# The last expert's remaining product rows: padded stationaries, no zero products, five ScalarE instructions

## The chip, the cores and the metric

The kernel runs on one core of one Trainium2 chip. The metric is the device time of one execution in microseconds (us); times are given as the median of several runs, and one further execution was profiled. The engines are TensorE (PE in the profile, with PEld for its weight loads), VectorE (DVE), ScalarE (ACT), GpSimd (POOL) and SyncE (SP).

## What is computed

Attention over 4 batches of 8 heads (768 positions, 64 columns each) with a causal mask in some heads and a sink-and-window mask in the others, and then a soft mixture of experts on its output. Only the second part bears on the change:

```python
logits = x @ phi                                  # 3072 x 32 slots
d = np.exp(logits - logits.max(0, keepdims=True)); d /= d.sum(0, keepdims=True) + 1e-09
slot_input = (d.T @ x).reshape(8, 4, 512)         # 8 experts, 4 slots each
for e in range(8):
    h = np.maximum(slot_input[e] @ w1[e], 0.0)    # 4 x 1024
    slot_out[e] = h @ w2[e]                       # 4 x 512
c = np.exp(logits - logits.max(1, keepdims=True)); c /= c.sum(1, keepdims=True) + 1e-09
return c @ slot_out.reshape(32, 512)              # 3072 x 512
```

## The kernel before

The program is a list of operations, each with a name, the engines it may run on, estimated costs, what it depends on and which buffers it takes and frees. A planner places them greedily by estimated start and a key, and emits each engine's instructions in that order; an engine then runs its instructions strictly in that order, and waits on semaphores for the others. Buffers in PSUM are five: two pairs of banks "sc", two banks "tr", one pair "pv". The planner also chooses the engine of an operation that allows two.

Attention runs over 16 pairs of batch and head group; GpSimd issues the loads of q, k, v and of the experts' matrices on one queue, so the matrices w1 and w2 arrive one after the other behind the attention's inputs. The last matrix, w2 of expert 7, comes in two pieces: row groups 0 to 5 (piece a) and 6 to 7 (piece b; FL is 6).

The tail, from the last attention pair on, goes so, with the lines of the profile:

- RC and RWR (L897, L898, L906): VectorE sums the exponentials into `rcs`, inverts it, and inverts the row sums into `rrow`.
- H, HR, TH, HE (L930, L940, L952, L279): the first expert layer for four experts at a time, the ReLU on ScalarE, the transposes, and the copies of the hidden rows into `hT_t` (tile xT), which VectorE does.
- W2.0 to W2.7 (L968): the second layer. Each expert's eight row groups are products of a stationary of only 32 columns (four slots of each of eight tiles), put into one of four column groups of the array, so that four run side by side; they add up in four 32-row strips of one "pv" bank. W2.7 does row groups 0 to 5 of the last expert, W2b later 6 and 7.
- SOa (L977): ScalarE scales the bank by `rcs` into `slot_out_a`, without row groups 6 and 7. SOb (L979): the same with them, on VectorE, into `slot_out`, after W2b.
- HG, GP, GE (L989, L999, L277 and L279): for the first 512 output rows the missing two row groups are brought in another way: the hidden rows times the exponentials, as a stationary `gT`.
- OG (L1027) and OM (L1023): the output products. For the first 512 rows an OG pair (gT with piece b) and an OM with `slot_out_a` add up in one bank; all later OM read `slot_out`.
- OE (L1041 on ScalarE, L1043 on VectorE): a bank is scaled by `rrow` into SBUF. ST (L1062): SyncE issues ten stores, four of 256 KB, two of 512 KB, four of 1 MB, each when its OE are done.

An order written out by hand (`seq`, L1052) chains OG and OM of the first rows, W2b and OM.1.0 on TensorE. Between W2.6 and W2.7 the two GP products stand.

After planning, products of a zero tile are put ahead of TensorE operations before which the plan has a gap, so that TensorE isn't idle (`zeros_for`, L1131). The count comes from the gap, and for operations whose name begins with "W2" it is at most 6:

```python
us, w = gap - (1.5 if o.name[:2] == "W2" else 0.12), 512 - c0
before[o.name] = (min(max(0, int(us / (w / 2400))), 6 if o.name[:2] == "W2" else 3), 0, bank, c0)
```

In the tail that puts five zero products of 512 columns, into the second "pv" bank, between GP and W2.7.

Of the kernel before, what the change touches and what calls it, by code (L numbers as in the profile page):

```python
# [15 lines left out]
ACT = mybir.ActivationFunctionType  # L16
# [159 lines left out]
def kernel(  # L176
# [13 lines left out]
    nc = tc.nc  # L190
    P = 128
    B, H, S, D = q.shape
# [22 lines left out]
    elg = sb.tile([P, 6, 4, NS], BF16, name="elg")  # L215
# [9 lines left out]
    rcs = sb.tile([P, 1], F32, name="rcs")  # L225
# [3 lines left out]
    thr = sb.tile([P, 2, H], F32, name="thr")  # L229
# [21 lines left out]
    pvb = ps.tile([P, 2, 512], F32, name="pv")  # L251

    def tr_bf(s, n):
        return trb[s].bitcast(BF16)[:, 0:n]
# [8 lines left out]
    NGT, FL, SOB = 4, 6, "DVE"  # L263
# [4 lines left out]
    hT_t = [xbf[:, 1024 * e:1024 * (e + 1)].rearrange("p (f c) -> p f c", f=8) for e in range(2)]  # L268

    pl = Plan({"S8": 11, "QT": 2, "KT": 2, "VT": 1, "VB": 2, "VF": 3, "PT": 2, "PTX": 2, "XB": 2,  # L270
               "XT": 1, "SC": 2, "TR": 2, "PV": 1})
# [3 lines left out]
    def copy(o, dst, src):  # L275
        if o.eng == "ACT":
            nc.scalar.copy(dst, src)  # L277
        else:
            nc.vector.tensor_copy(dst, src)  # L279
# [44 lines left out]
    NW, UNEVEN = 2 * NE, 5  # L324
    wbuf = [Buf("S8") for _ in range(NW)]
    wland = [None] * NW
    late_mem, last_lands = {}, []

    def w_view(i):
        m = late_mem[i]() if i in late_mem else slots[wbuf[i].slot][:, :]  # L330
        return m.rearrange("p (a f) -> p a f", a=4 if i < NE else 8)
# [84 lines left out]
    def head_mask(h):  # L416
        nc.vector.tensor_scalar(msk[:, h, 0:256], edist[:, 0:256], thr[:, 0, h:h + 1], None, op0=ALU.is_lt)
        nc.vector.tensor_scalar(msk[:, h, 256:896], edist[:, 256:896], thr[:, 1, h:h + 1], None, op0=ALU.is_lt)
# [54 lines left out]
    for n in range(4):  # L473
        o_hm[n] = [pl.op(f"hm{n}.{i}", {"DVE": 0.55}, -28.5 if n == 0 else T * n - 2.0, deps=[o_fl],
                         emit=lambda o, h=n + 4 * i: head_mask(h)) for i in range(2)]
# [15 lines left out]
    def emit_ph3(o):  # L491
        for n in range(4):
# [7 lines left out]
                  emit=lambda o: nc.vector.tensor_copy(phi.rearrange("p n s -> p (n s)"), tr_bf(phs[1].slot, 128)))  # L500
# [110 lines left out]
    def evs(x, b, n):  # L611
        if b == 0:
            return ev[x, b]
        return [e for r0, r1, e in ev[x, b] if r0 < 24 * (n + 1) and r1 > 24 * n]
# [15 lines left out]
    def mask_emit(b, n, m):  # L630

        def f(o):
            pT, mh = pTs[PTb[b, n].slot], msk[:, n::4, :]
            if m < 2:
                pw = pT[:, :, 1024 * m:1024 * (m + 1)].rearrange("p i (g c) -> p i g c", g=2)[:, :, :, 0:256]
                mw = (mh[:, :, 0:768].rearrange("p h (g c) -> p h g c", g=2)[:, :, :, 0:256] if m == 0 else
                      mh[:, :, 384:896].rearrange("p h (g c) -> p h g c", g=2))
            else:
                pw, mw = pT[:, :, 1920:2304], mh[:, :, 256:640]
            nc.vector.tensor_tensor(pw, pw, mw, op=ALU.mult)  # L640
        return f
# [6 lines left out]
    for b in range(B):  # L648
        for n in range(4):
            p = 4 * b + n  # L650
# [4 lines left out]
            def emit_v2(o, n=n, tr=tr):  # L655
                t = tr_bf(tr.slot, 768)
                for j in range(6):
# [4 lines left out]
                      emit=emit_v2)  # L662

            def emit_vb(o, b=b, n=n, tr=tr):
# [4 lines left out]
                           need=[VBb[b]], rel=[tr], emit=emit_vb)  # L669
            VFb[p] = Buf("VF")  # L670

            def emit_vf(o, b=b, n=n, p=p):
# [4 lines left out]
                           emit=emit_vf)  # L677

            PTb[b, n] = Buf("PT")
            for kk, g in enumerate(GORDER):  # L680
# [19 lines left out]
                if g in (1, 3, 4):  # L700
                    m = {1: 0, 3: 1, 4: 2}[g]
                    masko[p, m] = pl.op(f"MK.{p}.{m}", {"DVE": [0.70, 0.70, 0.57][m]}, key + 0.3,
                                        deps=[expo[p, x] for x in ((0, 1), (2, 3), (3, 4))[m]] + o_hm[n],
                                        emit=mask_emit(b, n, m))

        for ns in ([(0, 1), (2, 3)] if b == 0 else [(0, 1, 2, 3)]):
            sc = Buf("SC")

            def emit_lx(o, b=b, sc=sc, ns=ns):
# [4 lines left out]
                      deps=list(dict.fromkeys(e for n in ns for x in "qk" for e in evs(x, b, n))),  # L714
# [13 lines left out]
    xto, lgo, elo, elc, dso, eto = {}, {}, {}, {}, {}, {}  # L728
    dsm = {}
    for b in range(B):  # L730
        for n in range(4):
            p = 4 * b + n
# [4 lines left out]
            for i in iorder:  # L737
                deps, need = [v2e[p], vfo[p]], set()
# [6 lines left out]
                def emit_pv(o, b=b, n=n, p=p, i=i):  # L745
                    pT = pTs[PTb[b, n].slot]
                    vb = vbs[VBb[b].slot]
                    for h in range(2):
                        for j in range(i + 1):
# [3 lines left out]
                            else:  # L753
# [5 lines left out]
                             deps=list(dict.fromkeys(deps)) + ([last] if last else []),  # L759
# [17 lines left out]
            def emit_xt(o, b=b, n=n, tr=tr):  # L777
                t = tr_bf(tr.slot, 768)
                xv = xbs[XBb[b].slot]
                for i in range(6):  # L780
# [3 lines left out]
                      emit=emit_xt)  # L784
# [18 lines left out]
        else:  # L803
# [3 lines left out]
                           emit=lambda o, f=emit_lg: f(o, ns=(3,)))  # L807
# [8 lines left out]
        else:  # L816
            elo[b] = pl.op(f"EL.{b}", {"ACT": 0.35}, kb, deps=[lgo[b]], rel=[lg],
                           emit=lambda o, f=emit_el: f(o, c0=0, c1=1))
            elc[b] = pl.op(f"ELc.{b}", {"ACT": 0.67}, kb + 0.1, deps=[elo[b]], rel=[lg],
                           emit=lambda o, f=emit_el: f(o, c0=1, c1=4))  # L820
        dp = Buf("TR")

        def emit_ds(o, b=b, dp=dp):
            for i in range(6):
# [5 lines left out]
                  emit=emit_ds)  # L830
# [52 lines left out]
    kt = T * 16 + 10  # L883
# [12 lines left out]
    def emit_rc(o):  # L896
# [5 lines left out]
                  emit=emit_rw)  # L902
    o_rwb = pl.op("RWb", {"PE": 0.22}, kt - 1.7, n=8, deps=[o_rwa, eto[B - 1]], need=[cs],
                  emit=lambda o: emit_rw(o, (4, 5)))
    o_rw = pl.op("RWR", {"DVE": 0.25}, kt - 1.0, deps=[o_rwb], rel=[cs],
                 emit=lambda o: nc.vector.reciprocal(rrow, scb[cs.slot][:, 1, 0:24]))  # L906
    o_rc = pl.op("RC", {"DVE": 3.5}, kt + 24.0, deps=[eto[b] for b in range(B)], emit=emit_rc)
    si = Buf("TR")

    def emit_si(o):  # L910
        t = trb[si.slot][:, 0:4 * NS].rearrange("p (a s) -> p a s", a=4)
        sv = slot_sc.rearrange("p (di do) -> p do di", do=4)
        for do in range(4):
# [4 lines left out]
                  emit=lambda o: copy(o, siT.rearrange("p a s -> p (a s)"), trb[si.slot][:, 0:4 * NS]))  # L918
    hse, hte, w2o = {}, {}, []

    for e4 in range(2):
        hse[e4] = []
        for c in range(2):
            hp = Buf("SC" if c == 0 else "TR")
            bank = (lambda hp=hp: scb[hp.slot][:, 0, :]) if c == 0 else (lambda hp=hp: trb[hp.slot])
# [34 lines left out]
    so = Buf("PV")  # L960
    NL = NW - 1
    for e in range(NE):
        def emit_w2(o, e=e, fos=tuple(range(FL if e == NE - 1 else 8))):
            e4, g0 = e // 4, e % 4
            wv = w_view(NE + e)
            for fo in fos:
                g = fo % 4
                nc.tensor.matmul(pvb[32 * g:32 * (g + 1), 0, :], hT_t[e4][:, fo, 32 * g0:32 * (g0 + 1)],  # L968
                                 wv[:, fo, :], start=(e == 0 and fo < 4), stop=(e == NE - 1 and fo >= FL - 4),
                                 tile_position=(0, 32 * g), skip_group_check=True)  # L970
# [4 lines left out]
    def emit_so(o, d):  # L975
        if o.eng == "ACT":
            nc.scalar.activation(d, pvb[:, 0, :], ACT.Copy, scale=rcs[:, 0:1])  # L977
        else:
            nc.vector.tensor_scalar(d, pvb[:, 0, :], rcs[:, 0:1], None, op0=ALU.mult)  # L979

    so_a = pl.op("SOa", {"ACT": 0.69}, kt + 20, deps=[w2o[-1], o_rc], need=[so],
                 emit=lambda o: emit_so(o, slot_out_a))
    w2b = pl.op("W2b", {"PE": 0.11 + 0.11 * (8 - FL)}, kt + 29.0, n=8 - FL, deps=[so_a, last_lands[1]], need=[so],
                emit=lambda o: emit_w2(o, fos=tuple(range(FL, 8))))
    so_b = pl.op("SOb", {SOB: {"ACT": 0.69, "DVE": 0.74}[SOB]}, kt + 29.0, deps=[w2b], rel=[so],
                 emit=lambda o: emit_so(o, slot_out))

# [6 lines left out]
    for x in range(8 - FL):  # L994
# [3 lines left out]
        def emit_gp(o, x=x, gv=gv):  # L998
# [5 lines left out]
                        emit=lambda o, x=x, gv=gv: copy(o, gT[:, x, :], gv()[:, 0:128 * NGT])))  # L1004
# [8 lines left out]
    for m, (gi, r, d0, d1) in enumerate(parts):  # L1013
        c = ["SC", "TR", "SC", "TR"][m] if m < 4 else pat[(m - 4) % 5]
# [17 lines left out]
        if early:  # L1032
            og = [pl.op(f"OG.{gi}.{r}.{d0}", {"PE": 0.22 * (8 - FL) * (d1 - d0) / 512}, kt + 29 + 0.1 * m, n=8 - FL,
                        deps=[last_lands[1]] + ge, acq=[bf], emit=emit_og)]
        a = pl.op(f"OM.{gi}.{r}.{d0}", {"PE": 0.22 * (d1 - d0) / 512}, kt + 24 + m, n=1,
                  deps=og + [so_a if early else so_b], acq=[] if early else [bf], need=[bf], emit=emit_om)

        def emit_oe(o, gi=gi, r=r, d0=d0, d1=d1, bank=bank):
# [6 lines left out]
        w = (d1 - d0) / 512  # L1045
# [3 lines left out]
                  rel=[bf], emit=emit_oe))  # L1049

    tail = {o.name: o for o in pl.ops}
    seq = ["OG.0.0.0", "OM.0.0.0", "OG.0.0.256", "OM.0.0.256", "OG.0.1.0", "OM.0.1.0", "OG.0.2.0", "OM.0.2.0", "W2b",  # L1052
           "OG.0.3.0", "OM.0.3.0", "OM.1.0.0"]
    for x, y in zip(seq[:-1], seq[1:]):
        tail[y].deps.append(tail[x])
# [3 lines left out]
    for gi, r0, r1 in store_parts:  # L1059
        def emit_st(o, gi=gi, r0=r0, r1=r1):  # L1060
# [4 lines left out]
              emit=emit_st)  # L1065
# [21 lines left out]
    before, free, shift, hist = {}, 1.2, 0.0, []  # L1087
    for o in order:
        if o.eng != "PE":
            continue  # L1090
        if o is o_zb:
            hist += [(o.start + 0.30 * (x + 1), 512) for x in range(NZ)]
            free = o.end
            continue
        gap, at = max(o.start + shift - free, 0.0), free
        tail = at >= last_pv - 0.01 and o.start <= w_last.start + 0.01
        front = o.start <= 22.0
        if front:
            start = max(o.start + shift, free)
            slow = start < 4.2  # L1100
            unit = 0.427 if slow else 0.215
            n = int((gap - 0.1) / unit + 0.5) if gap > 0.2 else 0
            for _ in range(n):
                hist.append((free + unit, 512))
                free += unit
            took = (o.end - o.start) * (1.7 if slow else 1.0)
            while o.start > 4.5:
                e = max(free, o.start + shift) + took
                got = sum(a for t, a in hist if t > e - FW) + area(o.name)
                if got >= FA or n >= 6:  # L1110
                    break
                n += 1
                free += unit
                hist.append((free, 512))
            free = max(free, o.start + shift) + took
            hist.append((free, area(o.name)))
            if n:
                if at < first_pv:
                    before[o.name] = (n, 0, pvb[:, 1, :], 0)
            continue  # L1120
        free = o.end
        gap = o.start - at
        if gap < 0.6 or not tail:
            continue
        bank, c0 = (scb[1 - cs.slot] if o.start <= h_first + 0.01 else pvb)[:, 1, :], 0
        us, w = gap - (1.5 if o.name[:2] == "W2" else 0.12), 512 - c0
        before[o.name] = (min(max(0, int(us / (w / 2400))), 6 if o.name[:2] == "W2" else 3), 0, bank, c0)

    def zeros_for(n, m, bank, c0):
        for w in [512 - c0] * n + [128] * m:  # L1130
# [43 lines left out]
```

## Time and profile before

| | us |
|---|---|
| median of 3 runs (151.11 to 152.11) | 151.58 |
| the profiled execution | 151.7 |
| its span, first to last instruction | 149.9 |
| TensorE busy in it | 129.0 |
| VectorE busy | 114.3 |
| ScalarE busy | 109.5 |

The mean granted TensorE clock over the span is 0.978 of full speed. The share of busy time is a mean over stages: attention fills the first 117 us or so, the expert layers the next 12, the output products and their stores the rest. An instruction's row in the time line gives its start, its duration, engine, line, operation, the tile written and the tile read with partitions x elements, and a count where several are merged; in brackets stands how long the engine was idle before it, and which engine and line ended that. For matmuls, "128*32" is rows * columns of the array in use; their durations include the time through the array, so that the next one starts well before the end of the one ahead.

### The profile page before, as it was taken

What the parts mean: (1) busy time and instruction counts of PE and PEld (TensorE: products, weight loads), DVE (VectorE), ACT (ScalarE), POOL (GpSimd) and SP (SyncE); (2) the same over time, 40 slices, a digit from 0 to 9 for tenths busy, and PEclk for the clock granted to TensorE, in tenths of its full rate; (3) what the DMA queues carried; (4) which work ended last, traced back from release to release, by engine and by line L of the source; (5) the groups of instructions that cost most, each with busy time, mean ns of one, the idle gap of its engine ahead of it and who ended that gap; (6) DMA issues with size and microseconds to landing.
All of it is one profiled execution on the core that took longest, in us unless ns stands there. A gap on an engine that the chain in (4) does not pass through costs nothing.

```text
span 149.9 us, 4995 instructions
## 1 busy us (share of the span) xinstructions
PE 129.0 (86%) x2188; PEld 81.2 (54%) x2188; DVE 114.3 (76%) x242; ACT 109.5 (73%) x135; POOL 22.6 (15%) x46
## 2 busy tenths in 40 slices
PE   6999999889979899889999999899889799899000
PEld 2346556557757666667766766576664454333000
DVE  3697457996789889988999999899974873279300
ACT  3154399998988999999998999999981260469200
POOL 6911111411011220111200021101040000000000
PEclk9999999999999999999999999999999999999965
DMA  5999999999999999999999999999999998079994
GB/s 110 195 213 219 220 203 210 215 217 220 221 205 212 211 222 212 221 216 201 217 224 212 216 212 219 216 219 214 212 212 225 214 211 160 3 254 408 420 420 179
DMA packets 6872, 33.03 MB, mean 220 GB/s; under 512 B 819, under 2 KB 963, under 8 KB 4547
## 3 DMA queue, kind: packets, MB, share of 16 engines
q0 software_dynamic: 5120, 26.09, 85.4%
q1 hardware_dynamic: 1584, 6.55, 11.1%
q8 instruction: 17, 0.28, 0.7%
q10 hardware_dynamic: 146, 0.07, 0.2%
q14 instruction: 5, 0.04, 0.1%
HBM read 52.49 MB, written 6.29 MB: 392 GB/s over the span
## 4 chain that ended last, share of the span: by engine, by line
PE 53%; ACT 21%; DVE 15%; issue 3%; DVEq 1%; ACTq 0%
ACT pt L695 16%; PE sc L623 10%; PE pv L755 10%; PE pv L1131 6%; PE tr L595 5%; PE pv L457 4%; DVE xv L769 4%; PE pv L968 3%; DVE slot L1043 3%; PE tr L781 2%; DVE pt L640 2%; PE tr L796 2%; PE tr L658 2%; PE tr L553 1%; PE sc L930 1%
## 5 line engine op out<-in xcount | busy, mean ns | idle before, releaser
L695 ACT ACTIVATE pt<-sc 128x1024 bf16<-128x1024 f32 x80 | 76.6, 1044 | 3.0 <-PE sc L623 2.7
L623 PE MATMUL sc<-qk 64*128 64x512 bf16 (+3 forms) x256 | 31.4, 307 | 4.1 <-ACT pt L695 3.3
L640 DVE TENSOR_TENSOR pt<-pt,msk 128x1024 bf16<-128x1024 bf16 (+1 forms) x48 | 30.0, 638 | 0.1
L755 PE MATMUL pv<-vx,pt 128*128 128x65 bf16 x352 | 26.1, 193 | 0.5 <-DVE xv L769 0.4
L755 PEld LDWEIGHTS <-pt 128*128 128x128 bf16 x640 | 23.5, 97 | 5.5 <-issue 4.1
L755 PE MATMUL pv<-vf,pt 128*128 128x65 bf16 x288 | 21.1, 194 | 0.0
L623 PEld LDWEIGHTS <-qk 64*128 64x128 bf16 x256 | 10.5, 93 | 12.8 <-issue 7.4
L595 PE MATMUL tr<-ident,slot 128*64 128x128 bf16 (+1 forms) x448 | 16.1, 219 | 0.0
L279 DVE COPY qk<-tr 128x768 bf16<-128x768 bf16 (+2 forms) x26 | 14.0, 557 | 2.5 <-PE tr L595 1.8
L769 DVE TENSOR_TENSOR xv<-pv,rs 128x768 bf16<-128x768 f32 x16 | 15.3, 957 | 0.6
L595 PEld LDWEIGHTS <-slot 128*64 128x64 bf16 (+1 forms) x448 | 12.9, 110 | 4.4 <-issue 4.0
L284 POOL DMA_DIRECT2D slot<-in_moe_w_dram x15 | 8.1, 539 | 46.9 <-PE tr L595 18.3
L1131 PE MATMUL pv<-zero 128*128 128x512 bf16 x45 | 10.9, 381 | 0.0
L781 PE MATMUL tr<-ident,xv 128*128 128x128 bf16 x96 | 8.0, 219 | 2.2 <-DVE xv L769 0.8
L279 DVE COPY vx<-tr 128x768 bf16<-128x768 bf16 x14 | 7.6, 551 | 2.3 <-PE tr L658 2.3
L279 DVE COPY xT<-tr 128x768 bf16<-128x768 bf16 x14 | 7.7, 552 | 1.1 <-PE tr L781 1.1
L781 PEld LDWEIGHTS <-xv 128*128 128x128 bf16 x96 | 5.8, 97 | 4.7 <-issue 2.7
L279 DVE COPY xv<-tr 128x768 bf16<-128x768 bf16 (+2 forms) x15 | 6.4, 436 | 2.5 <-PE tr L553 2.2
L658 PE MATMUL tr<-ident,xv 128*128 128x128 bf16 x96 | 7.7, 219 | 0.1
L1131 PEld LDWEIGHTS <-zero 128*128 128x128 bf16 x53 | 4.5, 97 | 5.5 <-issue 1.3
L674 DVE TENSOR_TENSOR vf<-vx,fm 128x528 bf16<-128x528 bf16 x16 | 6.9, 429 | 0.5 <-ACT vx L277 0.3
L658 PEld LDWEIGHTS <-xv 128*128 128x128 bf16 x96 | 5.7, 97 | 1.9 <-issue 1.5
(127 smaller groups left out, 165.7 us busy)
## 6 DMA issues: line engine op xcount, KB each, us to landing
slot<-in_moe_w_dram POOLq DMA_DIRECT2D x9, 1024.0 KB, 19.9
out_dram<-slot SPq DMA_DIRECT2D x4, 1024.0 KB, 6.9
slot<-in_q_dram POOLq DMA_DIRECT2D x3, 768.0 KB, 19.4
slot<-in_k_dram POOLq DMA_DIRECT2D x3, 768.0 KB, 14.4
slot<-in_moe_w_dram POOLq DMA_DIRECT2D x2, 896.0 KB, 22.1
slot<-in_v_dram POOLq DMA_DIRECT2D x2, 768.0 KB, 12.6
slot<-in_v_dram POOLq DMA_DIRECT2D x2, 512.0 KB, 23.7
qk<-in_moe_w_dram POOLq DMA_DIRECT2D x1, 1024.0 KB, 14.5
```

The source lines that it names most:

```text
L279: nc.vector.tensor_copy(dst, src)
L284: emit=lambda o: nc.gpsimd.dma_start(dst(), src))
L595: nc.tensor.transpose(t[64 * i:64 * (i + 1), :, s, :], rv[:, i, 8 * c + s, :], ident[0:nr, 0:nr])
L623: nc.tensor.matmul(scb[sc.slot][:, i, c:c + 128 * nb], kk, qq.rearrange("p b c -> p (b c)"), start=True, stop=True)
L640: nc.vector.tensor_tensor(pw, pw, mw, op=ALU.mult)
L658: nc.tensor.transpose(t[:, 128 * j:128 * (j + 1)], vT[:, 6 * n + j, :], ident)
L674: nc.vector.tensor_tensor(vfs[VFb[p].slot], vv, fm[:, n], op=ALU.mult)
L695: nc.scalar.activation(pTs[PTb[b, n].slot][:, :, 512 * g:512 * (g + 1)], scb[sc.slot], ACT.Exp, scale=scale)
L755: nc.tensor.matmul(pvb[:, h, 65 * i:65 * (i + 1)], lt, rhs, start=(j == 0), stop=(j == i))
L769: nc.vector.tensor_tensor(xo, pvw[:, :, :, 0:64], r.rearrange("p i (j o) -> p i j o", o=1).to_broadcast([P, 2, 6, 64]), op=ALU.mult)
L781: nc.tensor.transpose(t[:, 128 * i:128 * (i + 1)], xv[:, i, 128 * n:128 * (n + 1)], ident)
L1131: nc.tensor.matmul(bank[:, c0:c0 + w], zero[:, 0:128], zero[:, 0:w], start=(c0 == 0), stop=True, skip_group_check=True)
```

## The change

Four things, in the tail alone.

First, W2b becomes WB. The last expert's two remaining row groups are multiplied with a stationary of the full 128 columns: a pad (`hpad`, in the memory of the spent tile elg), zero but for the 32 columns of the row group's strip. So the two products have the tiling of the output products beside them, and run over the whole "pv" bank instead of one strip each.

Second, the pad is made by HZ, a memset on VectorE once the last exponentials are transposed, and HP on ScalarE: two copies of 128 x 32 from `hT_t`, and behind them three copies of `rcs` into columns of the spent tile thr, which nothing reads.

Third, no zero products ahead of an operation whose name begins with "W2": the cap of 6 is 0.

Fourth, names and dependencies follow: WB waits for HP too, and its planned cost is 0.44 us where W2b's was 0.33.

```diff
-    w2b = pl.op("W2b", {"PE": 0.11 + 0.11 * (8 - FL)}, kt + 29.0, n=8 - FL, deps=[so_a, last_lands[1]], need=[so],
-                emit=lambda o: emit_w2(o, fos=tuple(range(FL, 8))))
+    hpad = elg.rearrange("p i o s -> p (i o s)")[:, 0:128 * (8 - FL)].rearrange("p (x c) -> p x c", c=128)
+    def emit_hp(o):
+        for x in range(8 - FL):
+            g = (FL + x) % 4
+            nc.scalar.copy(hpad[:, x, 32 * g:32 * (g + 1)], hT_t[1][:, FL + x, 96:128])
+        for x in range(NA):
+            nc.scalar.copy(thr[:, 1, x:x + 1], rcs)
+    o_hz = pl.op("HZ", {"DVE": 0.15}, kt + 2.5, deps=[eto[B - 1]], emit=lambda o: nc.vector.memset(hpad, 0.0))
+    NA = 3
+    o_hp = pl.op("HP", {"ACT": 1.1}, kt + 9, deps=[o_hz, hte[1], o_rc], emit=emit_hp)
+    def emit_w2b(o):
+        for x in range(8 - FL):
+            nc.tensor.matmul(pvb[:, 0, :], hpad[:, x, :], w_view(NW - 1)[:, FL + x, :], start=False, stop=True,
+                             skip_group_check=True)
+    w2b = pl.op("WB", {"PE": 0.22 * (8 - FL)}, kt + 29.0, n=8 - FL, deps=[so_a, o_hp, last_lands[1]], need=[so],
+                emit=emit_w2b)
...
-        before[o.name] = (min(max(0, int(us / (w / 2400))), 6 if o.name[:2] == "W2" else 3), 0, bank, c0)
+        before[o.name] = (min(max(0, int(us / (w / 2400))), 0 if o.name[:2] == "W2" else 3), 0, bank, c0)
```

In `seq`, "WB" stands where "W2b" stood. In the order that the planner makes of it, HP stands on ScalarE between the last HR and GE, HZ on VectorE ahead of the sum into `rcs`, TensorE has the same order without the five zero products and their weight loads, and from OM.1.0 on the evacuations OE are dealt out to ScalarE and VectorE in another pattern: 14 and 11 in place of 13 and 12.

More of the change, by code (lines that the diff above doesn't have):

```diff
@@ L1051 @@
     tail = {o.name: o for o in pl.ops}
-    seq = ["OG.0.0.0", "OM.0.0.0", "OG.0.0.256", "OM.0.0.256", "OG.0.1.0", "OM.0.1.0", "OG.0.2.0", "OM.0.2.0", "W2b",
+    seq = ["OG.0.0.0", "OM.0.0.0", "OG.0.0.256", "OM.0.0.256", "OG.0.1.0", "OM.0.1.0", "OG.0.2.0", "OM.0.2.0", "WB",
            "OG.0.3.0", "OM.0.3.0", "OM.1.0.0"]
```

## Prediction

> **What bounds the kernel now.** I read the page's slices first, then the chain that ended last, then the time line of TensorE, ScalarE and VectorE around the place where the slices go empty, and last the table by windows.
>
> ```profile
> PEclk9999999999999999999999999999999999999965
> DMA  5999999999999999999999999999999998079994
> GB/s 110 195 213 219 220 203 210 215 217 220 221 205 212 211 222 212 221 216 201 217 224 212 216 212 219 216 219 214 212 212 225 214 211 160 3 254 408 420 420 179
> ```
>
> These are the granted clock, the share of the DMA engines and their rate. A slice is 3.75 us. The DMA engines are full until slice 33, move almost nothing in slice 34 (127.4 to 131.2 us), and are full again to the end. The two full stretches are the loads and the stores. The hole between them is the time from the last weights to the first store, and it is bounded by computing, not by transfers. So what this change is worth is read from the hole, and from whether the stores then keep the engines full.
>
> ```profile
> 126.89 0.53 PE tr L999 x2
> 127.42 1.19 PE pv L1131 x5
> 128.60 0.56 PE pv L968 x6
> 129.16 0.02 issue
> 129.19 0.69 ACT msk L977
> 129.88 0.04 issue
> 129.92 0.27 PE sc L1023
> ```
>
> This is the chain of waits in order of time, inside the hole: GP (L999), five zero products (L1131), W2.7 (the last expert's first six products, L968), SOa (L977), and the first output product OM (L1023). The zero products stand on the chain. The next rows, of the time line, give the starts:
>
> ```profile
> 126.82 0.60 PE L999 MATMUL tr<-expT,msk 32*128 32x512 bf16 x2
> 127.35 1.25 PE L1131 MATMUL pv<-zero 128*128 128x512 bf16 x5
> 127.46 0.58 ACT L277 CAST msk<-tr 128x512 bf16<-128x512 f32 x1 [4.47 <-PE tr L999]
> 128.53 0.61 PE L968 MATMUL pv<-qk,xT 128*32 128x512 bf16 x6
> 129.07 0.39 PE L1027 MATMUL sc<-qk,msk 128*128 128x256 bf16 x2
> 129.19 0.69 ACT L977 ACTIVATE msk<-pv,rcs 128x512 bf16<-128x512 f32 x1 [1.14 <-PE pv L968]
> ```
>
> The weights that W2.7 and OG read come in two pieces; this is the view of their tile, the issues and then the times from issue to landing (least, median, most):
>
> ```profile
> L284 POOL DMA_DIRECT2D qk<-in_moe_w_dram x2: 528/532/536, 110.0 to 110.5; - x2
> ...
> DMA to landing us min/median/max: 17.0/17.4/17.8
> ```
>
> The pieces were issued at 110.0 and 110.5 and landed 17.0 and 17.8 us later: piece a (for W2.7) at 127.0, piece b (for the OG products, L1027) at 128.3. Piece a was there 0.35 us before the zero products even began.
>
> **The zero products: 1.18 us off the chain.** Five products take 1.25 with the last one running 0.38, so one starts (1.25 - 0.38) / 4 = 0.22 after another. GP's second starts at 126.82 + 0.22 = 127.04 and is through at 127.26; the zeros began 0.09 later. W2.7 also has another tiling than GP, and the switch into such a tiling costs 0.09 as well (131.44 + 0.22 = 131.66 against 131.75, rows below). So W2.7 starts at 127.35 instead of 128.53: 1.18 us earlier, with its weights landed at 127.0. What is late next? SOa starts 0.05 after W2.7's end (128.53 + 0.61 = 129.14, then 129.19), so at 128.01. ScalarE's copy GE (127.46, 0.58 us) ends at 128.04, and a following ScalarE operation may start some 0.1 us before the end of the one ahead (two of 0.69 take 1.26, below), so it doesn't hold SOa. SOa ends at 128.70, OM could start at 128.74. It needs OG's two products of 256 columns before it: piece b lands at 128.3, and OM can follow 0.22 after OG's first start, at 128.52. The cover is 0.2 us. So the first output, and with it the first store, comes 1.18 us earlier, at most 1.18 and less where the landings are later than in this execution.
>
> **W2b becomes WB: about +0.05 us.**
>
> ```profile
> 131.44 0.38 PE L1023 MATMUL tr<-msk,expT 128*128 128x512 bf16 x1
> 131.75 0.39 PE L968 MATMUL pv<-qk,xT 128*32 128x512 bf16 x2
> 132.07 0.61 PE L1027 MATMUL sc<-qk,msk 128*128 128x512 bf16 x2
> 132.25 0.75 DVE L979 TENSOR_SCALAR msk<-pv,rcs 128x512 bf16<-128x512 f32 x1 [0.29 <-PE pv L968]
> 132.93 0.69 ACT L1041 ACTIVATE slot<-sc,rrow 128x512 f32<-128x512 f32 x1 [0.39 <-PE sc L1023]
> 133.06 0.38 PE L1023 MATMUL pv<-msk,expT 128*128 128x512 bf16 x1 [0.17 <-DVE msk L979]
> 133.27 0.38 PE L1023 MATMUL tr<-msk,expT 128*128 128x512 bf16 x1
> 133.47 0.75 DVE L1043 TENSOR_SCALAR slot<-pv,rrow 128x512 f32<-128x512 f32 x1 [0.47 <-PE pv L1023]
> 133.69 1.26 ACT L1041 ACTIVATE slot<-tr,rrow 128x512 f32<-128x512 f32 x2
> ```
>
> Before, W2b's two products sit in different column groups and run side by side (0.39 us for both). Padded to all 128 columns they run one behind the other, 0.22 more. Without the change of tiling the first starts at 131.66 rather than 131.75, and the switch back (131.75 + 0.22 = 131.97 against 132.07, 0.10) goes too. On the old clock: WB at 131.66 and 131.88, through at 132.26, the next OG at 132.10 instead of 132.07. So 0.09 + 0.10 - 0.22 = -0.03: the new tiling buys nothing by itself on TensorE. The Trainium skill, page "TensorEngine Tiling (Array Packing)", section "Tiling Modes", says that changing the tiling mode drains the array. The rows agree only in part: a full drain would have let W2b start at 131.44 + 0.38 = 131.82, and it started at 131.75. By the rule the two switches would be worth 0.16 and 0.17, and the step would gain 0.11 in place of losing 0.03.
>
> SOb (L979) started 0.11 after W2b's end, where the other VectorE evacuation started 0.03 after its product (133.06 + 0.38 = 133.44, then 133.47). SOb waits for two engines before and for one in the changed program, so I take 0.04: SOb at 132.30, 0.05 later on the old clock (0.12 if the wait isn't what cost it, 0 if the profile's modelled ends flatter W2b).
>
> **Evacuations on other engines: about +0.12 us.** In the changed program's order the planner gives OM.1.0's evacuation to ScalarE and OM.1.1's to VectorE, the reverse of before. ScalarE is then still in OE.0.3 (132.93); it can start at 132.93 + 0.57 = 133.50 instead of VectorE's 133.47. OM.1.1 ends at 133.27 + 0.05 + 0.38 = 133.70, and its 0.75 on VectorE ends at 134.49, where ScalarE's 0.69 ended at 134.38. The fifth store needs both, so it comes 0.1 to 0.2 later against the shifted clock. Whether that reaches the end is in the table by windows (last columns: clock, DMA share, GB/s):
>
> ```profile
> 128.60:132.00 3.40, 2.94 (x21) 1.22 (x20) 1.24 (x2) 1.31 (x3) 0.00 (x0) 1.00 0.01 4
> 132.75:133.00 0.25, 0.14 (x1) 0.00 (x0) 0.25 (x1) 0.07 (x1) 0.00 (x0) 1.00 0.59 221
> 134.25:134.50 0.25, 0.25 (x3) 0.10 (x2) 0.25 (x1) 0.25 (x2) 0.00 (x0) 1.00 0.46 148
> 134.50:135.50 1.00, 0.94 (x4) 0.28 (x3) 1.00 (x3) 1.00 (x3) 0.00 (x0) 1.00 0.97 350
> 135.50:147.00 11.50, 3.28 (x12) 0.96 (x10) 4.65 (x8) 4.07 (x8) 0.00 (x0) 0.84 1.02 420
> 143.50:150.00 6.50, 0.00 (x0) 0.00 (x0) 0.00 (x0) 0.00 (x0) 0.00 (x0) 0.50 0.68 282
> ```
>
> From 135.5 on the DMA engines are full: nothing that computing does there counts. Before it there are two short gaps between stores; a later fifth store widens the second one, nearly one for one. SOb's 0.05 is part of the same delay. I count 0.15 for both (0 to 0.3).
>
> **The rest costs nothing, under cover.** For the zeroing of the pad (VectorE) and the five ScalarE instructions there is no such row; the nearest are:
>
> ```profile
> L452 DVE MEMSET zero<- x1: 272/272/272, 0.9 to 0.9; 128x256 uint32 x1
> ...
> 121.66 0.29 DVE L906 RECIPROCAL rrow<-sc 128x24 f32<-128x24 f32 x1
> 122.18 1.57 PE L952 MATMUL sc<-ident,msk 128*128 128x128 bf16 x16
> 123.86 0.69 DVE L279 COPY xT<-sc 128x1024 bf16<-128x1024 bf16 x1 [0.24 <-PE sc L952]
> ...
> L277 ACT CAST msk<-tr 128x128 bf16<-128x128 f32 x1 | 0.3, 265 | 1.3 <-PE tr L914 1.3
> ```
>
> The memset is half of one that took 0.27, so 0.1 to 0.27, and it is queued on VectorE ahead of the reduction and the two reciprocals. What waits behind it: the bank that the second reciprocal reads (done 121.95) is the one that the transposes at 122.18 write. The cover is 0.23 minus a hand-over of some 0.05; at the upper bound it costs 0.1, at my value of 0.15 nothing. The ScalarE five wait for the copy that ends at 123.86 + 0.69 = 124.55 and for the reciprocal; behind them on ScalarE stands GE, whose product comes at 127.46. Five at no more than 0.27 end by 125.9, with 1.5 us to spare. Below nothing neither can go: both only add.
>
> **Sum.** -1.18 + 0.15 = -1.0 us. On the profiled execution's 151.7 us (149.9 of span and 1.8 around it) that is 150.7; the median of the runs is 0.1 below that execution, so 150.6.
>
> **Rivals.** First, *the landings decide*. If the last weights come later than here, W2.7 waits for them and not for the zeros: over 0.35 us later for piece a, or over 0.2 for piece b, each further 0.1 us costs 0.1, up to the whole gain: 150.7 to 151.6. For it: the pieces stand at the end of a queue that is 17 us deep, and the three runs differ by 1.0 us. Against it: in this execution both were early enough. Chance 0.14.
>
> Second, on the other side, *the clock gate closes in the tail*. The zeros fed TensorE while it waited; without them its share of work in the hole falls. After the last product (in the 135.50 window) the granted clock was still 1.00 for a while and stood at 0.50 from 143.5 on. If it halves when W2.7 runs, the products from W2.7 to SOb (two rounds of W2.7, four products of 256 columns, eight of 512: about 2 x 0.22 + 4 x 0.11 + 8 x 0.22 = 2.6 us) take 2.6 us more: 151.6 - 1.0 + 2.6 = 153.2. It loses as soon as more than 1.0 us of such products is doubled. The Trainium skill, "TensorE: Matmul & The Clock Gate", section "A second HAM failure mode: psum-queue depth-cycling", says that short idles between groups of matmuls can be frequent enough for the gate to swing; no run here shows it. Against it: the stretch 128.6 to 132.0 keeps the clock at 1.00 with TensorE busy 2.94 of 3.40, and the changed tail has two idles (to 128.3 for piece b and to 128.74 for SOa) of 0.5 and 0.2 us. Chance 0.04.
>
> Third, *the tail gives the gain back*: the fifth store is later than I count, or SOb waits behind another evacuation on VectorE. Half to a whole evacuation there (0.35 to 0.75) leaves 0.3 to 0.7 of the gain: 150.9 to 151.3. Against it: VectorE sat idle for 0.29 before SOb and for 0.47 after it. Chance 0.10. That the change doesn't do what it says (zeros elsewhere on TensorE in their place) is excluded by the changed program's order: ten TensorE instructions fewer, none added.
>
> **Numbers.** My forecast, a gain of 0.8 to 1.2 us, gets the remaining 0.72. About 1% (1.5 us) is what a measurement of this kernel can tell from no change. The forecast lies 0.5 us short of 1% (150.06); with runs that spread over 1.0 us, one in five of its cases ends beyond: faster 0.15. Slower by over 1% is the gate's 0.04 and 0.02 for what I don't see. The range takes in the spread below the forecast and the landings above: 150.0 to 151.5.
>
> **What would show it.** In the changed profile: no zero product in the hole; W2.7 at about 127.35, SOa at 128.0, the first L1023 product at 128.74; slice 34 partly filled; the ScalarE five between 124.6 and 126; WB with no gap to its neighbours; a gap ahead of the fifth store that is up to 0.2 us wider than that of 134.25, then 420 GB/s. Wrong would be: W2.7 waiting for a DMA, a clock below 1.00 before the last product, or a second hole in the stores.

## The result, and the profile after

| | median | runs |
|---|---|---|
| before | 151.56 us (150.79 to 155.61) | 22 |
| changed | 150.29 us (149.84 to 153.33) | 22 |

The ratio of the changed kernel's time to the time before is 0.9938, with a 95% interval of 0.9915 to 0.996: about 0.9 us faster, 0.6 to 1.3 by the interval; the medians lie 1.27 us apart. The prediction was 150.6 us, in a range of 150.0 to 151.5.

The changed kernel was profiled three times. The first of these executions (153.3 us) is one of the slower ones at a lower granted clock, which the ratio leaves out: the last weights landed 2.4 us later than in the profile of before, and it is shown further below for what it tells. The lines here are of the third (150.0 us, span 148.2), called changed_third among the experiments. First the page: the span, then the slices of granted clock, DMA share and rate.

```profile
span 148.2 us, 4988 instructions
...
PEclk9999999999999999999999999999999999999855
DMA  5999999999999999999999999999999999269995
GB/s 110 200 212 217 217 209 212 212 212 228 217 202 215 215 218 214 212 221 201 213 219 229 217 212 215 214 217 212 212 217 215 219 218 187 53 243 396 420 416 226
```

The hole in slice 34 (now 126.0 to 129.7) is no longer empty: 53 GB/s where there were 3. That is no sign of an earlier store, though the prediction named it as one: the slice begins earlier and so takes in the last 0.18 MB of the loads, and the stores' data begins only behind it, at 130.58. The chain of waits, in order of time, and then the time line of the same stretch:

```profile
126.68 0.55 PE tr L1019 x2
127.23 0.02 issue
127.25 0.58 ACT msk L277
127.84 0.66 ACT msk L977
128.49 0.04 issue
128.54 0.27 PE sc L1043
```

```profile
124.38 0.34 ACT L989 COPY elg<-xT 128x32 bf16<-128x32 bf16 x2 [1.60 <-DVE xT L279]
124.62 0.37 ACT L992 COPY thr<-rcs 128x1 f32<-128x1 f32 x3
126.62 0.60 PE L1019 MATMUL tr<-expT,msk 32*128 32x512 bf16 x2
127.15 0.61 PE L968 MATMUL pv<-qk,xT 128*32 128x512 bf16 x6
127.80 0.69 ACT L977 ACTIVATE msk<-pv,rcs 128x512 bf16<-128x512 f32 x1
128.04 0.38 PE L1047 MATMUL sc<-qk,msk 128*128 128x256 bf16 x2 [0.28 <-DMA qk<-in_moe_w_dram]
128.54 0.27 PE L1043 MATMUL sc<-msk,expT 128*128 128x256 bf16 x1
130.05 0.38 PE L1043 MATMUL tr<-msk,expT 128*128 128x512 bf16 x1
130.26 0.59 PE L1000 MATMUL pv<-qk,elg 128*128 128x512 bf16 x2
130.70 0.59 PE L1047 MATMUL sc<-qk,msk 128*128 128x512 bf16 x2
130.90 0.75 DVE L979 TENSOR_SCALAR msk<-pv,rcs 128x512 bf16<-128x512 f32 x1 [0.33 <-PE pv L1000]
```

The zero products are gone from the chain. W2.7 (L968) starts 0.53 us behind GP (L1019), SOa 0.65 behind W2.7, and the first output product OM (L1043) 1.92 us behind GP, where it was 3.10 before: the 1.18 us that were counted. The chain now runs through ScalarE's copy GE (L277) and SOa, one right behind the other. The next thing to be late is already in sight: OG (L1047) waited 0.28 us for piece b of the weights. The five ScalarE instructions (L989, L992) took 0.6 us and were done 2.3 us before GE. WB (L1000) stands 0.21 behind the OM ahead of it, and the next OG 0.65 behind that OM (0.63 before).

### The profile page after: what moved, and what is told of

Same layout as the page of the kernel before. It is cut to its first block, busy times and chain, and to the rows that moved or that the text cites. A ratio compares the mean times of both kernels' runs of the same rounds, so it can differ in the third digit from the quotient of the medians.

```text
span 151.6 us, 4983 instructions
## 1 busy us (share of the span) xinstructions
PE 128.3 (85%) x2178; PEld 81.6 (54%) x2183; DVE 113.8 (75%) x242; ACT 110.7 (73%) x141; POOL 22.7 (15%) x46
## 4 chain that ended last, share of the span: by engine, by line
PE 45%; ACT 21%; DMA 13%; DVE 10%; issue 4%; ACTq 0%; POOL 0%; DVEq 0%
ACT pt L695 16%; DMA qk<-in_moe_w_dram 13%; PE sc L623 10%; PE pv L755 9%; PE tr L595 5%; PE pv L1151 5%; PE pv L457 4%; DVE xv L769 2%; PE tr L781 2%; PE tr L658 2%; DVE pt L640 1%; ACT slot L1061 1%; PE tr L553 1%; PE tr L796 1%; ACT vx L719 1%
## 5 line engine op out<-in xcount | busy, mean ns | idle before, releaser
L1151 PE MATMUL pv<-zero 128*128 128x512 bf16 x37 | 8.8, 380 | 0.3 <-issue 0.3
L1063 DVE TENSOR_SCALAR slot<-tr,rrow 128x512 f32<-128x512 f32 (+1 forms) x5 | 3.3, 691 | 5.0 <-PE tr L1043 5.0
```

The lines of the kernel that those rows point to most:

```text
L1151: nc.tensor.matmul(bank[:, c0:c0 + w], zero[:, 0:128], zero[:, 0:w], start=(c0 == 0), stop=True, skip_group_check=True)
```

## The experiments

All times are medians; the kernel before ran beside each group on the same chip, and the three groups ran on three chips. "Tail" below is the time from the first output product to the end of the span, and "head" the time from GP to the first output product.

**First group: the parts apart.** The changed kernel once more, and three variants: only the zero products taken out of the kernel before; the changed kernel with the zero products put back; the changed kernel without the three copies that nothing reads.

no_zeros_alone, against the kernel before:

```diff
-        before[o.name] = (min(max(0, int(us / (w / 2400))), 6 if o.name[:2] == "W2" else 3), 0, bank, c0)
+        before[o.name] = (min(max(0, int(us / (w / 2400))), 0 if o.name[:2] == "W2" else 3), 0, bank, c0)
```

pad_with_zeros, against the changed kernel:

```diff
-        before[o.name] = (min(max(0, int(us / (w / 2400))), 0 if o.name[:2] == "W2" else 3), 0, bank, c0)
+        before[o.name] = (min(max(0, int(us / (w / 2400))), 6 if o.name[:2] == "W2" else 3), 0, bank, c0)
```

without_three_copies, against the changed kernel:

```diff
-    NA = 3
+    NA = 0
```

> The changed kernel as it is, for a profile in which the last weights land as early as they did in the profile of before, and for its distance to the next three. By the prediction: W2.7 starts right behind GP, 0.53 us after GP's start, and not at the landing of piece a; SOa follows; the first output product starts 1.92 us after GP's start, where it was 3.10 before; 150.4 us. By the rival that the landings decide: W2.7 waits for a DMA again and the gain is under 0.7 us.

> The kernel before, with only the five zero products ahead of W2.7 left out. If the zero products are all that the change is worth (prediction: -1.18 us for them, +0.15 for the rest): 150.4 us, 0 to 0.15 us faster than the changed kernel. If the padded tiling brings something of its own (the drain rule: 0.1 to 0.3 us): 150.4 us too, but 0.1 to 0.3 us slower than the changed kernel.

> The changed kernel with the five zero products put back ahead of W2.7, so the pad, the full-width products and the five ScalarE instructions alone. Prediction: 0 to 0.3 us slower than the kernel before (151.6 to 151.9). If the padded tiling gains by itself: 0.1 to 0.3 us faster than before. In its profile WB's first product starts 0.22 us after the OM ahead of it (W2b: 0.31), and SOb 0.86 after that OM (W2b: 0.81).

> The changed kernel without the three copies of rcs that nothing reads; ScalarE then waits for VectorE again at SOa, as before. Prediction: no difference to the changed kernel (within 0.1 us), since those waits end over 4 us before SOa. If the copies are what speeds SOa: up to 0.1 us slower, and SOa later than 0.05 us after W2.7's end.

| kernel | us | ratio to before, 95% |
|---|---|---|
| before | 151.34 | |
| changed_again | 150.21 | 0.9938 (0.9912 to 0.9965) |
| no_zeros_alone | 150.37 | 0.9957 (0.9935 to 0.9979) |
| pad_with_zeros | 150.91 | 0.9982 (0.9961 to 1.0003) |
| without_three_copies | 150.20 | 0.9940 (0.9921 to 0.9958) |

Taking the zero products out gives 0.97 us by the medians (0.65 by the ratio, with an interval of 0.3 to 1.0), less than the 1.18 that stood on the chain. The time line of no_zeros_alone shows why:

```profile
125.57 0.60 PE L999 MATMUL tr<-expT,msk 32*128 32x512 bf16 x2
126.82 0.61 PE L968 MATMUL pv<-qk,xT 128*32 128x512 bf16 x6 [0.65 <-DMA qk<-in_moe_w_dram]
...
129.05 0.38 PE L1027 MATMUL sc<-qk,msk 128*128 128x256 bf16 x2 [1.62 <-DMA qk<-in_moe_w_dram]
```

In this execution TensorE reached GP 1.2 us earlier than in the profile of before (125.57 against 126.82), and the weights did not come earlier with it: W2.7 waited 0.65 us for piece a and OG 1.62 for piece b. The head took 129.27 - 125.57 = 3.70 us, longer than with the zero products. In changed_again it was 3.30, and in without_three_copies, where mainly OG waited, 2.15. So behind the zero products stands the landing of the last weights. In this execution the zero products would have cost nothing: with the 3.10 of before the first output product would have come at 128.67, and piece b held it to 129.27.

pad_with_zeros was to be 0 to 0.3 us slower than before and was 0.43 faster by the medians, with an interval that just takes in no change. Its time line answers for the tiling:

```profile
130.88 0.38 PE L1043 MATMUL tr<-msk,expT 128*128 128x512 bf16 x1
131.10 0.59 PE L1000 MATMUL pv<-qk,elg 128*128 128x512 bf16 x2
131.53 0.59 PE L1047 MATMUL sc<-qk,msk 128*128 128x512 bf16 x2
131.73 0.75 DVE L979 TENSOR_SCALAR msk<-pv,rcs 128x512 bf16<-128x512 f32 x1 [0.33 <-PE pv L1000]
```

WB starts 0.22 behind the OM (W2b 0.31), OG follows 0.65 behind it (0.63), SOb 0.85 (0.81): as expected, nothing is gained there. The gain comes behind all that. Its tail is 149.0 - 129.37 = 19.6 us, against 149.9 - 129.92 = 20.0 before, although the same bytes are stored. That of without_three_copies is 20.0, that of changed_again 19.7. So in these profiles the three copies that nothing reads go with a tail shorter by 0.3 us, on an engine that waits for TensorE there. The times don't show it: without_three_copies took 150.20 us and changed_again 150.21, no difference, as was expected.

What differs is seen in the DMA queues. These are the queues of before in the half microsecond from 134.7 on (queue, packets, MB, share of the 16 engines), and of without_three_copies from 133.3 to 133.9:

```profile
q1 hardware_dynamic: 88, 0.17, 91.8%
q14 instruction: 1, 0.01, 3.8%
```

```profile
q1 hardware_dynamic: 104, 0.21, 97.0%
q14 instruction: 1, 0.01, 4.2%
```

One packet of instructions is fetched while the stores (q1) already fill the engines. In changed_third the same packet comes between 129.5 and 130.5, ahead of the stores' data, which begins at 130.58:

```profile
q14 instruction: 1, 0.01, 3.3%
```

Nothing but three ScalarE instructions differs between without_three_copies and the changed kernel, so it is ScalarE's code, and more instructions ahead of that point bring its fetch forward. What the fetch costs shows at the other end, in the last stretch of the stores by windows (last columns: clock, DMA share, GB/s), first of before, then of without_three_copies, then of changed_third:

```profile
131.95:147.95 16.00, 6.60 (x25) 2.13 (x23) 7.43 (x12) 7.16 (x12) 0.00 (x0) 0.85 0.98 393
147.95:148.50 0.55, 0.00 (x0) 0.00 (x0) 0.00 (x0) 0.00 (x0) 0.00 (x0) 0.50 0.04 15
```

```profile
146.84:147.23 0.39, 0.00 (x0) 0.00 (x0) 0.00 (x0) 0.00 (x0) 0.00 (x0) 0.50 0.06 21
```

```profile
130.58:146.58 16.00, 6.53 (x25) 2.11 (x23) 6.77 (x10) 7.61 (x13) 0.00 (x0) 0.78 0.98 393
146.58:146.75 0.17, 0.00 (x0) 0.00 (x0) 0.00 (x0) 0.00 (x0) 0.00 (x0) 0.50 0.05 0
```

A share of 0.04 to 0.06 is about one engine of 16 (1/16 = 0.06) with the rest idle: before, one DMA engine finishes its part of the stores 0.55 us behind the others, in without_three_copies 0.39. The reading is that this is the engine that fetched the packet, and that it carries the delay to the end. The profile doesn't name the engine of a packet, so this link is inferred; the packet itself took 0.3 us (3.8% of 16 engines for 0.5 us), less than the lag. The last store's data does bound the end: the span ends 1.4 us behind it in both (148.50 and 149.9, 146.75 and 148.2). In changed_third the last stretch moves almost no bytes, and the stores are through 16.17 us after their first packet (130.58 to 146.75) in place of 16.55 (131.95 to 148.50).

**Second group: the code fetch by itself.** Theory A is that the added ScalarE instructions, and not the padded tiling, make the tail shorter. five_copies_alone is the kernel before with five copies that nothing reads; five_copies_no_zeros is the same without the zero products; pad_zeros_two_copies is pad_with_zeros with NA = 0.

```diff
+    def emit_hp(o):
+        for x in range(5):
+            nc.scalar.copy(thr[:, 1, x:x + 1], rcs)
+
+    pl.op("HP", {"ACT": 1.1}, kt + 9, deps=[hte[1], o_rc], emit=emit_hp)
...
```

> The kernel before, zero products and W2b included, with only five ScalarE copies of rcs that nothing reads, where the changed kernel has its five. In the profile of before a small instruction fetch falls at 134.8, among the stores, and one DMA engine ends 0.5 us behind the others; in the two profiles with all five added ScalarE instructions it falls ahead of the stores (130.8 and 130.7) and none lags. Theory A, the added instructions move ScalarE's code fetch ahead of the stores: 0.3 to 0.5 us faster than before, first store to last data 16.2 us instead of 16.5. Theory B, what pad_with_zeros gained is the tiling's: no difference to before.

> The same without the five zero products: the two parts that theory A counts, W2b unpadded. Theory A: as fast as the changed kernel or up to 0.1 us faster (150.1), since the pad itself gains nothing. Theory B: 0.2 to 0.4 us slower than the changed kernel, as no_zeros_alone.

> The changed kernel with the zero products back and without the three copies of rcs: the pad, its two ScalarE copies and the full-width products. Theory A: the code fetch falls three ScalarE instructions later, among the stores, a DMA engine lags by 0.3 us, and pad_with_zeros' gain of 0.4 is mostly gone (0 to 0.2 faster than before). Theory B: as fast as pad_with_zeros, 0.4 faster than before.

| kernel | us | ratio to before, 95% |
|---|---|---|
| before | 151.45 | |
| five_copies_alone | 151.15 | 0.9980 (0.9958 to 1.0002) |
| five_copies_no_zeros | 150.05 | 0.9926 (0.9900 to 0.9952) |
| pad_zeros_two_copies | 151.11 | 0.9982 (0.9959 to 1.0005) |

The medians alone decide little: five copies gain 0.3 us and the interval just takes in no change; pad_zeros_two_copies was to have lost most of pad_with_zeros' gain and was 0.34 faster than before, at the same ratio as pad_with_zeros (0.9982). five_copies_no_zeros is as fast as the changed kernel, as theory A has it, and 0.3% ahead of no_zeros_alone, though the intervals overlap. The profiles separate the theories in the tail, since head and tail can be read apart:

| profile | zeros | ScalarE added | W2b or WB | head | tail |
|---|---|---|---|---|---|
| before | 5 | 0 | W2b | 3.10 | 20.0 |
| pad_zeros_two_copies | 5 | 2 | WB | 3.10 | 20.0 |
| pad_with_zeros | 5 | 5 | WB | 3.11 | 19.6 |
| five_copies_alone | 5 | 5 | W2b | 3.10 | 19.6 |
| no_zeros_alone | 0 | 0 | W2b | 3.70 | 20.1 |
| without_three_copies | 0 | 2 | WB | 2.15 | 20.0 |
| changed_again | 0 | 5 | WB | 3.30 | 19.7 |
| changed_third | 0 | 5 | WB | 1.92 | 19.7 |
| five_copies_no_zeros | 0 | 5 | W2b | 2.16 | 19.5 |
| five_copies_no_zeros_2 | 0 | 5 | W2b | 1.92 | 19.6 |

(changed_third and five_copies_no_zeros_2 belong to the third group.) The tail is 19.5 to 19.7 with five added instructions and 20.0 to 20.1 with none or two, whatever stands in for W2b. In every row with five the fetch lies ahead of the stores, in every row with none or two among them. Three profiles of kernels with five are not in the table: the two with late weights of the third group have 19.7 as well, and the first one of the changed kernel has 20.4, with the clock at 0.50 in the first 1.35 us of it. The head is 3.10 or 3.11 in every row with zero products, and without them 1.92 to 3.70, as the weights land. In five_copies_alone the packet and the last stretch of the stores read:

```profile
q14 instruction: 1, 0.01, 3.7%
```

```profile
148.40:148.55 0.15, 0.00 (x0) 0.00 (x0) 0.00 (x0) 0.00 (x0) 0.00 (x0) 0.50 0.03 0
```

The packet was read in the window 131.6 to 132.4, alone; the stores' data starts at 132.47, and no engine lags at the end. Theory B falls: the tail shortens without the pad. What the times leave open is how much of that reaches the whole: without the pad, five copies gain 0.3 to 0.8 us by the ratios (0.9980 against 1, and 0.9926 and 0.9904 against 0.9957), and in the padded kernels the three copies gain nothing (0.9938 and 0.9940, 0.9982 and 0.9982), where the tails would have it 0.3.

**Third group: late weights, and the pad's price.** In the first profile of the changed kernel the first two rivals of the prediction, late landings and the clock gate, are seen at once. These are its time line at W2.7, its windows, and the landings of the last two pieces:

```profile
126.82 0.60 PE L1019 MATMUL tr<-expT,msk 32*128 32x512 bf16 x2
...
129.44 1.04 PE L968 MATMUL pv<-qk,xT 128*32 128x512 bf16 x6 [2.02 <-DMA qk<-in_moe_w_dram]
```

```profile
129.20:132.60 3.40, 2.73 (x13) 1.28 (x14) 0.30 (x1) 1.16 (x2) 0.00 (x0) 0.50 0.02 4
132.60:140.00 7.40, 7.01 (x28) 2.64 (x28) 5.99 (x10) 5.78 (x10) 0.00 (x0) 1.00 0.77 292
```

```profile
L284 POOL DMA_DIRECT2D qk<-in_moe_w_dram x2: 531/534/536, 110.0 to 110.5; - x2
...
DMA to landing us min/median/max: 19.4/19.8/20.2
```

Piece a landed at 129.4 rather than 127.0, TensorE waited 2.02 us for it, and the granted clock stood at 0.50 for 3.4 us from 129.2 on, so that W2.7 took 1.04 us in place of 0.61. The DMA share was 0.05 from 128.4 to 130.6, about one engine of 16: here, too, one engine ended behind the others, with the loads; why is not shown. Would the zero products have kept the clock? Two kernels delay the last matrix by one more load, one without and one with zero products (the cap is 6 again, and the planner puts six):

```diff
+    dma("w16", -16.5, 1 << 20, 128, None,
+        lambda: qk_mem[QTb[3].slot][:, 8 * KB:12 * KB].rearrange("p (a f) -> p a f", a=4),
+        moe_w2[NE - 1].rearrange("(fi fo) d -> fi fo d", fo=8)[:, 0:4, :], deps=qk_done[3])
     load_w(15, -16, deps=qk_done[3])
```

Beside them, the changed kernel and five_copies_no_zeros were timed once more on one chip.

> The changed kernel with one more load of 1 MB (half of the last matrix again, into memory that nothing reads) queued ahead of the last matrix, so that both pieces land some 2.4 us later and W2.7 waits for piece a. That wait is some 2 us of idle TensorE without zero products. Gate theory: as in the first profile of the changed kernel, where the clock stood at 0.50 from 129.2 for 3.4 us, the gate closes in most executions, W2.7 takes 1.04 us instead of 0.61, and the tail is 0.5 to 1.1 us longer than in late_weights_zeros. Rival, the idle is too short for the gate and what was slow there was the landing alone: the same time as late_weights_zeros within 0.2 us. Both: slower than the changed kernel by 1.5 to 3.5 us.

> The same extra load with zero products ahead of W2.7 (the planner now puts six, 1.3 us, which the wait for piece a covers). Gate theory: the clock stays at 1.00 to the end of the products, and the kernel is 0.5 to 1.1 us faster than late_weights_no_zeros. Rival: no difference to it within 0.2 us.

> Once more beside the changed kernel on one chip: no zero products, five idle ScalarE copies, W2b unpadded. By the profiles, from the first output product to the end it takes 19.53 us and the changed kernel 19.65: 0.1 us faster than the changed kernel. If the padded products help, slower than it.

> The changed kernel as it is, on the same chip as the three above: 1.2 us faster than before, 0 to 0.2 us slower than five_copies_no_zeros_2.

| kernel | us | ratio to before, 95% |
|---|---|---|
| before | 151.42 | |
| late_weights_no_zeros | 154.21 | 1.0145 (1.0098 to 1.0191) |
| late_weights_zeros | 154.27 | 1.0163 (1.0125 to 1.0202) |
| five_copies_no_zeros_2 | 150.00 | 0.9904 (0.9878 to 0.9929) |
| changed_third | 150.07 | 0.9916 (0.9889 to 0.9943) |

The two late kernels agree within 0.06 us, and the gate theory's 0.5 to 1.1 us for the zero products isn't there. Both are 4.1 to 4.2 us slower than the changed kernel by the medians, where 1.5 to 3.5 were expected. In both, the executions lie in two groups, at 152.5 to 153.3 us with a mean granted clock of 0.972 to 0.975, and at 154.2 to 154.8 with 0.961 to 0.964; the lower clock fits one stretch of 3.4 us at half speed (3.4 x 0.5 / 151 = 0.011). So the clock falls in the late case, but with six zero products as often as without: in four of six executions either way. Both profiles caught the other group, where TensorE waited and the clock stayed; this is W2.7 in each, first without zero products and then with:

```profile
129.28 0.61 PE L971 MATMUL pv<-qk,xT 128*32 128x512 bf16 x6 [1.57 <-DMA qk<-in_moe_w_dram]
```

```profile
130.47 0.61 PE L971 MATMUL pv<-qk,xT 128*32 128x512 bf16 x6 [1.70 <-DMA qk<-in_moe_w_dram]
```

That the zero products are an insurance for late weights is not shown; whether they would be for a wait somewhat shorter than here was not tried.

The last pair is too close for its times (150.00 and 150.07). By the profiles five_copies_no_zeros has the shorter tail, by 0.1 us, which is what the padded products and the other pattern of evacuations cost together. Its ratios, 0.9926 and 0.9904, lie 0.001 (0.2 us) under the changed kernel's 0.9938 and 0.9916, inside the intervals. So a version with no pad at all is at least as fast, and that it is faster is not shown.

## Why the prediction was right, and where not

**The zero products.** Right in mechanism and, where the weights are early, in size: the first output product comes 1.92 us behind GP in changed_third, as worked out. Too large in the mean: of the seven profiles of kernels without zero products and without an extra load, three (changed_again, no_zeros_alone and the first one) had W2.7 waiting 0.65 to 2.02 us for piece a. In two more (without_three_copies and five_copies_no_zeros) W2.7 started 0.65 and 0.69 us behind GP in place of 0.53, just as piece a landed, and OG waited for piece b. The prediction took the landing from one profile and gave later ones a chance of 0.14; they are common, and no_zeros_alone puts what they took back at 0.2 us by its median (1.18 less 0.97) and 0.5 by its ratio.

**WB and the evacuations.** Right: WB at 0.21 to 0.22 behind the OM (0.22 said), the OG behind it at 0.65 (0.66 said), SOb at 0.85 (0.86 said). The fifth store was to come 0.1 to 0.2 later against the shifted clock: its issue comes 4.61 us behind the first output product in changed_third (133.15) and came 4.48 behind it before (134.40). The tails with five added instructions put the price of all this at about 0.1 us (19.6 to 19.7 with WB, 19.5 to 19.6 with W2b), where 0.15 was counted; the tails with none or two (20.0 to 20.1 either way) don't show it. What the prediction took for the switch of tiling, 0.09 to 0.10 and not a full drain, held: pad_with_zeros gained nothing on TensorE from losing two switches (OG 0.65 behind the OM, 0.63 before).

**The five ScalarE instructions.** This is the step that failed, as the prediction put it: "Below nothing neither can go: both only add." Their own time was hidden, 0.6 us with 2.3 us to spare. But they move ScalarE's next code fetch out of the stores, which is worth 0.3 to 0.5 us in the tails of the profiles. The quoted argument looked at the engine's time and at who waits behind it, and not at what else an instruction occupies: a place in the code, and so the time of a transfer on the DMA engines that bound the end.

**The sum.** The forecast of -1.0 us was met by -0.9 to -1.3, and that is partly luck: the landings took back 0.2 to 0.5 of the zero products' gain, and the code fetch, not counted, shortened the tail by 0.3 to 0.5. How much of this second part is in the changed kernel's median stays open, since its time without the three copies is the same.

**The rivals.** The landings do decide in part of the profiled executions. The clock gate did close once in a profile of the changed kernel, as the rival had it, at 0.50 for 3.4 us; but it closed during a wait of 2 us for weights and not in the thinner tail, and in changed_third the clock is 1.00 throughout the tail's products. Nor is a low clock peculiar to kernels without zero products: one execution of five_copies_alone, which has them, took 153.05 us at a mean clock of 0.966. The tail did not give the gain back.

## What to carry to other kernels

Where transfers bound the end of a kernel, read every queue in the stretch that they fill, the instruction queues too: with one packet of code among the stores the tail was 0.3 to 0.5 us longer here, and five ScalarE instructions that nothing needs moved the packet away. An instruction count is an input to the schedule, so an edit "hidden under cover" can still change the end, in either direction; test it with instructions that do nothing. When a filler is taken off a chain, look at several profiles for what stands behind it: here a landing that one profile showed early held W2.7 for 0.65 us or more in three of seven others.

## What the runs showed of the hardware

A small instruction packet among stores that fill the DMA engines goes with one engine lagging at the end: with the packet at 134.7 to 135.2, one engine was 0.55 us behind the others at 148.5, over 13 us later, and with the packet ahead of the stores none was. That the delay starts with the packet is inferred, since the profile doesn't name its engine. In the first profile of the changed kernel the pieces of the last matrix took 19.4 and 20.2 us from issue to landing, where they had taken 17.0 and 17.8.

The granted clock fell to 0.50 at 129.20 in the first profile of the changed kernel, 1.8 us after GP's end and during TensorE's wait of 2.02 us, and rose again after one stretch of 3.4 us; waits of 1.57 us (late_weights_no_zeros) and 1.70 (late_weights_zeros) left it at 1.00. What decides between the two was not settled.

A switch of the array's tiling took 0.09 to 0.10 us, and the first product after it (131.75 in the profile of before) began before the one ahead had ended (131.82), so the rule "Mode switching requires drain" of the Trainium skill, page "TensorEngine Tiling (Array Packing)", section "Tiling Modes", was worth less here than a full drain.

On code fetches the Trainium skill, page "Runtime: NRT & Kernel Launch", section "Instruction fetch mechanics", says that the cost of crossing a block boundary is one DMA tail-bump, mostly hidden. For the engine that runs the code the trace of before agrees: around the fetch at 134.8 ScalarE's evacuations follow one another without a gap (134.84, 135.41, 136.55). For the transfers that share the DMA engines the traces show a cost: 0.3 to 0.5 us in the tail.
